# Transposes released by a small DMA on the sixth x tile, scalars without square roots on ScalarE, skip inputs loaded ahead of stores

## The chip, the cores and the metric

The kernel runs on one core of one Trainium2 chip. The metric is device time in microseconds (us) from start to end of one execution. A core has TensorE (PE in the profile; PEld is its weight loading), VectorE (DVE), ScalarE (ACT), GpSimd (POOL) and SyncE (SP). SP computes nothing here: it issues DMAs, and it issues them in the order of its queue, so that an issue that waits holds up all behind it.

## What is computed

A gate mixes two branches over the same input `x` of 2048 rows and 1024 columns, in bfloat16:

```python
g = sigmoid((x * gate_w).sum(-1, keepdims=True))
a = irfft2(rfft2(x) * (w_r + 1j * w_i))               # branch A: a filter in frequency
dt = exp(log_dt); Lam = Lambda_re + 1j * Lambda_im
Lam_bar = exp(dt * Lam)
B_bar = ((Lam_bar - 1.0) / Lam)[:, None] * Bmat
h[t] = Lam_bar * h[t - 1] + x[t] @ B_bar.T            # branch B: a state of 1024 complex numbers
b = 2.0 * real(h @ Cmat.T) + x * Dskip
out = g * a + (1 - g) * b
```

## The kernel before

**Branch A.** The Fourier transforms are matrix products with constant matrices. `fstage` (jj of 0 to 7) takes one x tile of 128 partitions x 2 x 1024: DVE forms sums and differences of halves (`eo`), POOL the few edge columns, and after every second tile PE does 4 groups of products into `ps_f`, each copied from PSUM into `big` (as `FX`) by two casts, L476 and L477. `fd`, `bf_w` and `bi` then go over 16 groups g of frequencies: forward along the columns (`ps_d`), forward along the rows (`ps_xe`, `ps_xo`), the product with the filter W on DVE, and back (`ps_q`). `idm` and `fi` transform back along the columns and write branch A's result to a scratch in HBM (`ya_scratch`). Each g needs a matrix MM that SP loads (L232) and a W that POOL loads.

**Branch B.** Time is cut into 4 chunks c of 512 steps, the 1024 states into 4 quarters q. `ssm_pe` multiplies x, transposed (`xT`), with B, transposed (`BT`), into `psu`; ACT scales the result by `rho` or `nrho` into `u`, of which there are two buffers. `ssm_dve` turns u by a phase from a table `tab`, runs four scans (L408), and turns the result back into `h`. A unit of this is one (c, q); there are 16. `tables(q)` makes the table of a quarter during chunk 0, from `thp`, `beta` and a ramp. `rho`, `nrho`, `thp`, `beta` and `r_sb` come from a chain of operations on 128 x 8 numbers (L278 to L344), with four table loads on ACT: for Exp, for Sin, for Sqrt, and for Sin and Arctan.

**Output.** For each tile tb of 128 rows, `half` multiplies h with C, transposed (`CT`), into `psy`, in two halves of 16 matmuls; L789 then forms `o` = psy x (1 - g) + `xf`, and SP stores it (L791). `xf` is prepared by `prep_d` (DVE: `xc` = x tile times Dskip, L760) and `prep_a` (ACT: `gac` = branch A's tile times g, L764; `xf` = xc times 1 - g, L766; POOL then adds gac to xf by an accumulating DMA, L767). At its end `prep_a` issues on SP the loads of xc and gac two tiles ahead. There are two buffers for xc and o, three for gac and xf.

**What sets the order.** Within the first stages SP and POOL, in the last stage ACT and SP, keep the order in which the program is written; the other engines' order is settled by a scheduler when the program is built, and each engine then runs its list in order. Two generators are merged by their planned times: branch A beside branch B's chunk 0 and part of the next, then branch B beside `c_all`, which writes out the order of the halves and what is prepared after each (`pre`).

**The start.** SP loads the x tiles, the first transform matrix `G_sb`, MM and W. Then come DMA transposes of B and of x. They are written after the fifth `fstage`; the first of them overwrites a place in BT into which POOL copies one column of the eighth x tile, so it must wait for that copy (L678):

```python
nc.gpsimd.tensor_copy(out=BT[:, 0, 0, 0, 0:1], in_=xts[7][:, 0, 0:1])
load_BT(0)
load_xT(0)
load_M(1)
...
```

Of the kernel before, what the change touches and what calls it, by code (L numbers as in the profile page):

```python
# [22 lines left out]
P = 128  # L23
# [113 lines left out]
def kernel(  # L137
# [137 lines left out]
    lre, lim, ldt = vec[:, 0, :], vec[:, 1, :], vec[:, 2, :]  # L275
    chpi = sp.tile([P, 1], FP32, name="chpi")
    nc.vector.memset(chpi, HALF_PI)
    dt = v8("dt")  # L278
    nc.scalar.activation(out=dt, in_=ldt, func=ACT.Exp)
    are = v8("are"); nc.vector.tensor_mul(out=are, in0=dt, in1=lre)  # L280
    r_sb = v8("r_sb")
    nc.scalar.activation(out=r_sb, in_=are, func=ACT.Exp)
    thp = v8("thp")
    nc.vector.scalar_tensor_tensor(out=thp, in0=lim, scalar=INV2PI, in1=dt, op0=ALU.mult, op1=ALU.mult)

    def frac(xx, n, nm, pool=sp, tag=None):
        kk = pool.tile([P, n], FP32, name=nm + "_k", **({"tag": tag} if tag else {}))
        nc.vector.tensor_scalar(out=kk, in0=xx, scalar1=MAGIC, scalar2=-MAGIC, op0=ALU.add, op1=ALU.add)
        nc.vector.tensor_sub(out=xx, in0=xx, in1=kk)
        nc.vector.tensor_scalar(out=kk.bitcast(I32), in0=xx.bitcast(I32), scalar1=0x7FFFFFFF, scalar2=None,  # L290
                                op0=ALU.bitwise_and)
        return xx, kk

    ang = sp.tile([P, 16], FP32, name="ang")
    nc.vector.tensor_copy(out=ang[:, 0:8], in_=thp)
    nc.vector.tensor_scalar_mul(out=ang[:, 8:16], in0=thp, scalar1=float(TC))
    rr, ra = frac(ang, 16, "ang")
    snc = sp.tile([P, 2, 16], FP32, name="snc")

    den = v8("den"); nc.vector.tensor_mul(out=den, in0=lre, in1=lre)  # L300
    den2 = v8("den2"); nc.vector.tensor_mul(out=den2, in0=lim, in1=lim)
    nc.vector.tensor_add(out=den, in0=den, in1=den2)
    inv = v8("inv"); nc.vector.reciprocal(out=inv, in_=den)
    nc.scalar.activation(out=snc[:, 0, :], in_=rr, func=ACT.Sin, scale=TWO_PI_LO)
    nc.scalar.activation(out=snc[:, 1, :], in_=ra, func=ACT.Sin, scale=-TWO_PI_LO, bias=chpi)
    sth, cth, sTC, cTC = snc[:, 0, 0:8], snc[:, 1, 0:8], snc[:, 0, 8:16], snc[:, 1, 8:16]
    sg = sp.tile([P, 8, 2], FP32, name="sg")
    nc.vector.tensor_scalar_mul(out=sg[:, :, 1], in0=sTC, scalar1=-1.0)
    nc.vector.tensor_copy(out=sg[:, :, 0], in_=sTC)
    lbi = v8("lbi"); nc.vector.tensor_mul(out=lbi, in0=r_sb, in1=sth)  # L310
    nr = v8("nr"); nc.vector.tensor_mul(out=nr, in0=r_sb, in1=cth)
    nc.vector.tensor_scalar_add(out=nr, in0=nr, scalar1=-1.0)
    t_a = v8("t_a"); nc.vector.tensor_mul(out=t_a, in0=nr, in1=lre)
    t_b = v8("t_b"); nc.vector.tensor_mul(out=t_b, in0=lbi, in1=lim)
    cr = v8("cr"); nc.vector.tensor_add(out=cr, in0=t_a, in1=t_b)
    t_c = v8("t_c"); nc.vector.tensor_mul(out=t_c, in0=lbi, in1=lre)
    t_d = v8("t_d"); nc.vector.tensor_mul(out=t_d, in0=nr, in1=lim)
    ci = v8("ci"); nc.vector.tensor_sub(out=ci, in0=t_c, in1=t_d)
    m2 = v8("m2"); nc.vector.tensor_mul(out=m2, in0=cr, in1=cr)
    m3 = v8("m3"); nc.vector.tensor_mul(out=m3, in0=ci, in1=ci)  # L320
    nc.vector.tensor_add(out=m2, in0=m2, in1=m3)
    mag = v8("mag")
    nc.scalar.activation(out=mag, in_=m2, func=ACT.Sqrt)
    rho = v8("rho")
    nc.vector.scalar_tensor_tensor(out=rho, in0=mag, scalar=2.0, in1=inv, op0=ALU.mult, op1=ALU.mult)
    nrho = v8("nrho")
    nc.vector.tensor_scalar_mul(out=nrho, in0=rho, scalar1=-1.0)
    hd = v8("hd"); nc.vector.tensor_add(out=hd, in0=mag, in1=cr)
    nc.vector.tensor_scalar_max(out=hd, in0=hd, scalar1=1e-30)
    nc.vector.reciprocal(out=hd, in_=hd)  # L330
    ht = v8("ht"); nc.vector.tensor_mul(out=ht, in0=ci, in1=hd)
    nc.vector.tensor_scalar(out=ht, in0=ht, scalar1=-1e15, scalar2=1e15, op0=ALU.max, op1=ALU.min)
    hq = v8("hq"); nc.vector.tensor_mul(out=hq, in0=ht, in1=ht)
    nc.vector.tensor_scalar_add(out=hq, in0=hq, scalar1=1.0)
    nc.scalar.activation(out=hq, in_=hq, func=ACT.Sqrt)
    nc.vector.tensor_scalar_add(out=hq, in0=hq, scalar1=1.0)
    nc.vector.reciprocal(out=hq, in_=hq)
    nc.vector.tensor_mul(out=ht, in0=ht, in1=hq)
    nc.scalar.activation(out=hd, in_=ht, func=ACT.Sin)
    fq = v8("fq")  # L340
    nc.scalar.activation(out=fq, in_=ht, func=ACT.Arctan)
    beta = v8("beta")
    nc.vector.tensor_scalar_mul(out=beta, in0=thp, scalar1=-255.5)
    nc.vector.scalar_tensor_tensor(out=beta, in0=fq, scalar=-2.0 * INV2PI, in1=beta, op0=ALU.mult, op1=ALU.add)  # L344

    tau_i = rp.tile([P, TC], I32, name="tau_i", tag="su")
    nc.gpsimd.iota(tau_i, pattern=[[1, TC]], base=0, channel_multiplier=0)
# [2 lines left out]

    def tables(q):
        xa = rp.tile([P, 2 * TC], FP32, name="xa", tag="cu")
        for jj in range(2):
            jb = 2 * q + jj
            xj = xa[:, TC * jj:TC * (jj + 1)]
            if q < 2:
                nc.vector.tensor_scalar(out=xj, in0=tau_f, scalar1=thp[:, jb:jb + 1], scalar2=beta[:, jb:jb + 1],
                                        op0=ALU.mult, op1=ALU.add)
            else:
                nc.scalar.activation(out=xj, in_=tau_f, func=ACT.Identity, scale=thp[:, jb:jb + 1],  # L360
                                     bias=beta[:, jb:jb + 1])
        rr, ra = frac(xa, 2 * TC, "xa", rp, "su")
        tq = tab[:, 2 * q:2 * q + 2]
        rr = rr.rearrange("p (a t) -> p a t", a=2)
        ra = ra.rearrange("p (a t) -> p a t", a=2)
        nc.scalar.activation(out=tq[:, :, 0, :], in_=ra, func=ACT.Sin, scale=-TWO_PI_LO, bias=chpi)
        nc.scalar.activation(out=tq[:, :, 1, :], in_=rr, func=ACT.Sin, scale=-TWO_PI_LO)
        nc.vector.tensor_scalar_mul(out=tq[:, :, 2, :], in0=tq[:, :, 1, :], scalar1=-1.0)


    hs = {}
# [71 lines left out]
    def fstage(jj):  # L443
# [10 lines left out]
        nc.gpsimd.tensor_sub(out=eo[:, :, 1, 1, 0:1], in0=om, in1=eo[:, :, 1, 0, 0:1])  # L454
        nc.gpsimd.tensor_add(out=eo[:, :, 1, 0, 0:1], in0=om, in1=eo[:, :, 1, 0, 0:1])
        eos[jj] = eo
        if jj % 2 == 0:
            return
        j0 = 2 * jj - 2
        for eo_i in range(2):  # L460
            for b in range(2):
                ps = psF.tile([P, 4, 2, P], FP32, name="ps_f", tag="ps")
                bs = slice(P * b, P * (b + 1))
                for jl in range(4):
# [9 lines left out]
                                     start=False, stop=True)  # L474
                q = 4 * eo_i + 2 * b
                nc.scalar.copy(out=FX[:, q, :, j0:j0 + 4], in_=ps[:, :, 0, :].rearrange("p j c -> p c j"))  # L476
                (nc.vector.tensor_copy if (eo_i, b) in ((1,0),(1,1)) else nc.scalar.copy)(  # L477
                    out=FX[:, q + 1, :, j0:j0 + 4], in_=ps[:, :, 1, :].rearrange("p j c -> p c j"))
                yield 1.0

# [193 lines left out]
    for jj in range(8):  # L674
        for _ in fstage(jj):
            pass
        if jj == 4:
            nc.gpsimd.tensor_copy(out=BT[:, 0, 0, 0, 0:1], in_=xts[7][:, 0, 0:1])  # L678
            load_BT(0)
            load_xT(0)  # L680
            load_M(1)
            load_W(1)
            load_BT(1)
            load_M(2)
            nc.sync.dma_start(out=FI_sb, in_=cFI)
            load_BT(2)
            load_BT(3)

    def ssm_all():
        prev = iter(())  # L690
        for c in range(NCH):
            for q in range(4):
                if c == 0:
                    tables(q)
                u = up.tile([P, 2, 2, TC], BF16, name="u", tag="u")
                for i, _ in enumerate(ssm_pe(c, q, u)):
                    yield 0.5
                    for _ in range((0,4,3,3)[i]):
                        next(prev, None)
                        yield 0.52  # L700
                prev = ssm_dve(c, q, u)
        for _ in prev:
            yield 0.72
# [29 lines left out]
    with ExitStack() as bctx:  # L733
# [59 lines left out]
        def c_all():  # L793
            order = [(0, 0), (1, 0), (2, 0), (0, 1), (1, 1), (2, 1)] + [(tb, dh) for tb in range(3, 16) for dh in range(2)]
            pre = {(0, 0): [(prep_d, 0), (prep_d, 1)], (1, 0): [(prep_a, 0)], (2, 0): [(prep_a, 1)],
                   (0, 1): [(prep_d, 2)], (1, 1): [(prep_a, 2)], (2, 1): [(prep_d, 3)], (3, 0): [(prep_a, 3), (prep_d, 4)],
                   (3, 1): [(prep_a, 4)]}
            for n in range(5, 16):
                pre[n - 1, 0] = [(prep_d, n)]
                pre[n - 1, 1] = [(prep_a, n)]  # L800
            for tb, dh in order:
                half(tb, dh)
                for f, n in pre.get((tb, dh), ()):
                    f(n)
                yield 3.6

        while ssm.t < 48:
# [38 lines left out]
```

## Time and profile before

| | |
|---|---|
| median of 6 runs | 353.71 us (351.27 to 356.54) |
| the profiled execution | 351.27 us |
| its span, first to last instruction | 349.5 us |
| mean granted TensorE clock | 0.993 |
| PE busy | 324.0 us (93%) |
| DVE busy | 297.6 us (85%) |
| ACT busy | 188.1 us (54%) |
| POOL busy | 42.2 us (12%) |

Times inside the execution are counted from the start of the span. Busy time of PE is modelled from pipelined matmuls, so that a busy PE is not PE at its peak. A wait is put down to what came last of all that the instruction waited for. In the row of activity each digit is the busy share of one fortieth of the span, in tenths.

### The profile page before, as it was taken

Reading aid. Unit: us, or ns where it says so; the run is one execution under the profiler, and the core shown is the slowest. Engines: PE = TensorE matmul, PEld = TensorE weight load, DVE = VectorE, ACT = ScalarE, POOL = GpSimd, SP = SyncE. Lnnn points to the kernel's source line nnn. Section 1 sums busy time; section 2 is a strip of 40 time slices with the busy share of each in tenths; the row PEclk is TensorE's granted clock in tenths of the full one; section 3 lists DMA queues with packets and bytes.
Section 4 is the critical chain, followed back from the end, with each engine's and each line's share of the span. In section 5 each row is a group of like instructions: output and inputs, shape, how many; then the busy total and the mean of one; then the engine's idle time right before and its main releaser. Section 6 shows DMA issues by size and latency. Waiting matters only on the chain.

```text
span 349.5 us, 4890 instructions
## 1 busy us (share of the span) xinstructions
PE 324.0 (93%) x1804; PEld 172.9 (49%) x1804; DVE 297.6 (85%) x419; ACT 188.1 (54%) x255; POOL 42.2 (12%) x89
## 2 busy tenths in 40 slices
PE   3788999799979999999999999999989898999995
PEld 1675666466646566554444444444434343444442
DVE  4998859978999969898999999989799798987431
ACT  1997979689948877596262426242322404322430
POOL 5330422122110000000011000000000000000110
PEclk9999999999989999999999999999999999999999
DMA  7899997989694121113994145223523223454863
GB/s 279 342 138 217 220 249 192 188 182 202 179 222 90 71 112 62 60 60 137 239 251 128 37 143 148 64 90 84 128 55 96 92 60 113 99 143 130 266 200 105
DMA packets 68169, 51.30 MB, mean 147 GB/s; under 512 B 52657, under 2 KB 55729, under 8 KB 68145
## 3 DMA queue, kind: packets, MB, share of 16 engines
q1 hardware_dynamic: 64144, 38.75, 44.7%
q0 software_dynamic: 3648, 12.07, 14.1%
q8 instruction: 14, 0.23, 0.3%
q10 hardware_dynamic: 352, 0.17, 0.2%
q14 instruction: 11, 0.08, 0.1%
HBM read 21.61 MB, written 8.39 MB: 86 GB/s over the span
## 4 chain that ended last, share of the span: by engine, by line
PE 56%; DVE 21%; DMA 9%; ACT 8%; issue 4%; SPq 2%; POOL 0%; DVEq 0%; ACTq 0%; POOLq 0%
PE psy L782 26%; PE psu L388 19%; DVE su L408 7%; DMA xc<-in_A_x_dram 3%; PE ps_id L557 3%; DVE cu L403 2%; DVE cu L433 2%; ACT X L500 2%; DMA CT<-in_A_x_dram 2%; DMA xT<-in_A_x_dram 1%; PE ps_d L488 1%; DMA MM<-c_MM 1%; DVE o L789 1%; ACT u L390 1%; ACT X L515 1%
## 5 line engine op out<-in xcount | busy, mean ns | idle before, releaser
L388 PE MATMUL psu<-xT,BT 128*128 128x512 bf16 x512 | 120.5, 379 | 5.9 <-ACT u L390 4.5
L388 PEld LDWEIGHTS <-BT 128*128 128x128 bf16 x512 | 49.7, 98 | 61.7 <-issue 7.6
L408 DVE TENSOR_TENSOR_SCAN su<-r_sb,carry,cu 128x512 bf16<-128x512 f32 x48 | 57.7, 1265 | 0.4
L390 ACT ACTIVATE u<-psu,rho 128x512 bf16<-128x512 f32 x32 | 22.1, 690 | 65.5 <-PE psu L388 35.5
L767 POOL DMA_DIRECT2D xf<-gac x16 | 14.0, 872 | 216.8 <-ACT xf L766 203.8
L782 PEld LDWEIGHTS <-h 128*128 128x128 bf16 x256 | 25.0, 98 | 30.2
L390 ACT ACTIVATE u<-psu,nrho 128x512 bf16<-128x512 f32 x32 | 22.1, 691 | 29.0 <-PE psu L388 29.0
L764 ACT ACTIVATE gac<-gac,gf 128x1024 bf16<-128x1024 bf16 x16 | 18.3, 1142 | 27.8 <-DMA gac<-ya_scratch 27.8
L782 PE MATMUL psy<-CT,h 128*128 128x512 bf16 x128 | 28.9, 379 | 0.0
L782 PE MATMUL psy<-big,h 128*128 128x512 bf16 x128 | 28.9, 379 | 0.0
L760 DVE TENSOR_TENSOR xc<-xc,dsk_bc 128x1024 bf16<-128x1024 bf16 x16 | 11.0, 687 | 18.5 <-DMA xc<-in_A_x_dram 18.5
L789 DVE SCALAR_TENSOR_TENSOR o<-psy,om_f,xf 128x1024 bf16<-128x1024 f32 (+1 forms) x17 | 20.6, 1215 | 6.9 <-PE psy L782 6.9
L399 DVE TENSOR_TENSOR cu<-u,tab 128x2048 bf16<-128x2048 bf16 x16 | 19.5, 1220 | 5.1 <-ACT u L390 5.1
L550 ACT CAST big<-ps_q 128x1024 bf16<-128x1024 f32 x16 | 16.4, 1027 | 10.2 <-PE ps_q L549 10.1
L782 PEld LDWEIGHTS <-big 128*128 128x128 bf16 x128 | 12.5, 98 | 15.1
L782 PEld LDWEIGHTS <-xT 128*128 128x128 bf16 x128 | 12.5, 98 | 15.1
L546 PE MATMUL ps_q<-MM,Y 128*128 128x256 bf16 x64 | 15.7, 279 | 4.6 <-DVE Y L527 4.6
L403 DVE TENSOR_TENSOR cu<-cu,su 128x2048 bf16<-128x2048 bf16 x16 | 19.6, 1226 | 0.3
L433 DVE TENSOR_TENSOR cu<-su,tab 128x2048 bf16<-128x2048 bf16 x16 | 19.5, 1220 | 0.1
L435 DVE TENSOR_TENSOR u<-su,tab 128x2048 bf16<-128x2048 bf16 x16 | 19.5, 1220 | 0.0
L401 DVE TENSOR_TENSOR su<-u,tab 128x2048 bf16<-128x2048 bf16 x16 | 19.5, 1219 | 0.0
L488 PE MATMUL ps_d<-G_sb,big 128*128 128x256 bf16 (+3 forms) x128 | 18.8, 286 | 0.0
(168 smaller groups left out, 558.8 us busy)
## 6 DMA issues: line engine op xcount, KB each, us to landing
xf<-gac POOLq DMA_DIRECT2D x16, 512.0 KB, 3.9
ya_scratch<-ya SPq DMA_DIRECT2D x16, 256.0 KB, 2.0
xc<-in_A_x_dram SPq DMA_DIRECT2D x16, 256.0 KB, 2.9
gac<-ya_scratch SPq DMA_DIRECT2D x16, 256.0 KB, 3.0
out_dram<-o SPq DMA_DIRECT2D x15, 256.0 KB, 2.0
MM<-c_MM SPq DMA_DIRECT2D x16, 192.0 KB, 3.9
xt<-in_A_x_dram SPq DMA_DIRECT2D x4, 512.0 KB, 4.2
CT<-in_A_x_dram SPq DMA_DIRECT2D x4, 512.0 KB, 8.0
```

The costliest lines, as they stand in the source:

```text
L388: nc.tensor.matmul(psu, lhsT=BT[:, jb, ri, dblk, :], rhs=xT[:, dblk, TC * c:TC * (c + 1)], start=(dblk == 0), stop=(dblk == 7))
L390: nc.scalar.activation(out=u[:, jj, ri, :], in_=psu, func=ACT.Copy, scale=(nrho if ri else rho)[:, jb:jb + 1])
L399: nc.vector.tensor_mul(out=cu, in0=u, in1=tq[:, :, 0:1, :].to_broadcast(full))
L401: nc.vector.tensor_mul(out=su, in0=u[:, :, ::-1, :], in1=tq[:, :, 1:3, :])
L403: nc.vector.tensor_add(out=cu, in0=cu, in1=su)
L408: nc.vector.tensor_tensor_scan(out=su[:, jj, ri, :], data0=r_sb[:, jb:jb + 1].to_broadcast([P, TC]), data1=cu[:, jj, ri, :], initial=(0.0 ...
L433: nc.vector.tensor_mul(out=cu, in0=su, in1=tq[:, :, 0:1, ::-1].to_broadcast(full))
L435: nc.vector.tensor_mul(out=u, in0=su[:, :, ::-1, :], in1=tq[:, :, 1:3, ::-1])
L488: nc.tensor.matmul(ps[:, lo:lo + w], lhsT=FX[:, q, 8 * g:8 * g + 8, :], rhs=G_sb[:, o:o + w], start=start, stop=stop, skip_group_check=True)
L764: nc.scalar.activation(out=gac, in_=gac, func=ACT.Copy, scale=gf[:, tb:tb + 1])
L782: nc.tensor.matmul(psy[:, ds], lhsT=hs[c, jb // 2][:, jb % 2, ri, P * tq:P * (tq + 1)], rhs=CT[dh][:, jb, ri, :], start=(i == 0), stop=(i ...
L789: nc.vector.scalar_tensor_tensor(out=o[:, ds], in0=psy[:, ds], scalar=om_f[:, tb:tb + 1], in1=xfs[tb][:, ds], op0=ALU.mult, op1=ALU.add)
```

## The change

*Release.* The POOL copy goes; instead SP moves 16 numbers of one partition of the sixth x tile into BT by a DMA, ahead of the transposes.

*Scalars.* The chain is rewritten as a generator `scalars()`, of which one step is taken before the first `fstage` and one in each of the following. The two Sqrt activations are replaced by an inverse square root on DVE (a first value from the bits of the number, then two Newton steps), the half-angle formula changes so that one Sin goes too, real and imaginary parts are handled in one operation of 16 columns, and a few operations move to POOL (`nrho`, a first `beta`, `sg`, the squared modulus).

*Casts.* In `fstage` the second cast of each group is always ACT's; before, DVE did it in two of the four.

*Tables.* `tables(q)` becomes a generator that treats its two halves of 512 columns one after the other.

*Skip inputs.* In `c_all` what is prepared comes before a `half` and no longer after it, and from tile 4 on `prep_a(n)` and `prep_d(n + 1)` stand together at (n - 1, 1). The loads that `prep_a` issues so stand on SP ahead of the store of that half's tile.

```diff
+    def rsqrt(y, x, s):
+        nc.vector.tensor_scalar(out=y.bitcast(I32), in0=x.bitcast(I32), scalar1=-0.5, scalar2=float(0x5F3759DF),
+                                op0=ALU.mult, op1=ALU.add)
+        for _ in range(2):
+            nc.vector.tensor_mul(out=s, in0=y, in1=y)
+            nc.vector.scalar_tensor_tensor(out=s, in0=s, scalar=-0.5, in1=x, op0=ALU.mult, op1=ALU.mult)
+            nc.vector.scalar_tensor_tensor(out=y, in0=s, scalar=1.5, in1=y, op0=ALU.add, op1=ALU.mult)
...
-    nc.scalar.activation(out=mag, in_=m2, func=ACT.Sqrt)
+        rsqrt(rs, m2, s)
+        nc.vector.tensor_mul(out=mag, in0=m2, in1=rs)
+        yield
+        nc.vector.scalar_tensor_tensor(out=rho, in0=mag, scalar=2.0, in1=inv, op0=ALU.mult, op1=ALU.mult)
+        nc.gpsimd.tensor_scalar_mul(out=nrho, in0=rho, scalar1=-1.0)
...
-    nc.scalar.activation(out=hq, in_=hq, func=ACT.Sqrt)
...
-    nc.scalar.activation(out=hd, in_=ht, func=ACT.Sin)
...
+    chain = scalars()
+    for _ in range(1):
+        next(chain, None)
...
     def tables(q):
         xa = rp.tile([P, 2 * TC], FP32, name="xa", tag="cu")
+        kk = rp.tile([P, 2 * TC], FP32, name="xa_k", tag="su")
+        tq = tab[:, 2 * q:2 * q + 2]
         for jj in range(2):
...
+            nc.scalar.activation(out=tq[:, jj, 0, :], in_=kj, func=ACT.Sin, scale=-TWO_PI_LO, bias=chpi)
+            nc.scalar.activation(out=tq[:, jj, 1, :], in_=xj, func=ACT.Sin, scale=-TWO_PI_LO)
...
         eos[jj] = eo
+        for _ in range(1):
+            next(chain, None)
...
-                (nc.vector.tensor_copy if (eo_i, b) in ((1,0),(1,1)) else nc.scalar.copy)(
+                (nc.vector.tensor_copy if (jj, eo_i, b) in () else nc.scalar.copy)(
...
         if jj == 4:
-            nc.gpsimd.tensor_copy(out=BT[:, 0, 0, 0, 0:1], in_=xts[7][:, 0, 0:1])
+            nc.sync.dma_start(out=BT[0:1, 0, 0, 0, 0:16], in_=xts[5][0:1, 0, 0:16])
             load_BT(0)
...
-                   (0, 1): [(prep_d, 2)], (1, 1): [(prep_a, 2)], (2, 1): [(prep_d, 3)], (3, 0): [(prep_a, 3), (prep_d, 4)],
-                   (3, 1): [(prep_a, 4)]}
-            for n in range(5, 16):
-                pre[n - 1, 0] = [(prep_d, n)]
-                pre[n - 1, 1] = [(prep_a, n)]
+                   (0, 1): [(prep_d, 2)], (1, 1): [(prep_a, 2)], (2, 1): [(prep_d, 3)], (3, 0): [(prep_a, 3), (prep_d, 4)]}
+            for n in range(4, 16):
+                pre.setdefault((n - 1, 1), []).append((prep_a, n))
+                if n < 15:
+                    pre.setdefault((n - 1, 1), []).append((prep_d, n + 1))
             for tb, dh in order:
-                half(tb, dh)
                 for f, n in pre.get((tb, dh), ()):
                     f(n)
+                half(tb, dh)
                 yield 3.6
```

More of the change, by code (lines that the diff above doesn't have):

```diff
@@ L277 @@
     nc.vector.memset(chpi, HALF_PI)
[L278 to L287, printed above, removed]
+    r_sb, beta, rho, nrho = (v8(n) for n in ("r_sb", "beta", "rho", "nrho"))
@@ L288, in frac @@
+    ang = sp.tile([P, 16], FP32, name="ang")
+    angk = rp.tile([P, 2, 16], FP32, name="angk", tag="cu")
+    snc = sp.tile([P, 2, 16], FP32, name="snc")
+    thp = ang[:, 0:8]
+    sTC, cTC = snc[:, 0, 8:16], snc[:, 1, 8:16]
+    sg = sp.tile([P, 8, 2], FP32, name="sg")
+    lam = scr[:, 28:30, :]
+    def frac(xx, kk, ff):
         nc.vector.tensor_scalar(out=kk, in0=xx, scalar1=MAGIC, scalar2=-MAGIC, op0=ALU.add, op1=ALU.add)
-        nc.vector.tensor_sub(out=xx, in0=xx, in1=kk)
-        nc.vector.tensor_scalar(out=kk.bitcast(I32), in0=xx.bitcast(I32), scalar1=0x7FFFFFFF, scalar2=None,
+        nc.vector.tensor_sub(out=ff, in0=xx, in1=kk)
+        nc.vector.tensor_scalar(out=kk.bitcast(I32), in0=ff.bitcast(I32), scalar1=0x7FFFFFFF, scalar2=None,
@@ L291, in frac @@
                                 op0=ALU.bitwise_and)
[L292 to L322, printed above, removed]
-    nc.scalar.activation(out=mag, in_=m2, func=ACT.Sqrt)
[L324 to L334, printed above, removed]
-    nc.scalar.activation(out=hq, in_=hq, func=ACT.Sqrt)
@@ L336, with v16 @@
-    nc.vector.tensor_scalar_add(out=hq, in0=hq, scalar1=1.0)
-    nc.vector.reciprocal(out=hq, in_=hq)
-    nc.vector.tensor_mul(out=ht, in0=ht, in1=hq)
-    nc.scalar.activation(out=hd, in_=ht, func=ACT.Sin)
[L340 to L344, printed above, removed]
+    def v16():
+        scr_n[0] += 2
+        return scr[:, scr_n[0] - 2:scr_n[0], :]
@@ new lines, in rsqrt, with scalars @@
+    def rsqrt(y, x, s):
[5 more added lines that the diff above has]
+            nc.vector.scalar_tensor_tensor(out=y, in0=s, scalar=1.5, in1=y, op0=ALU.add, op1=ALU.mult)
+    def scalars():
+        dt, are = v8("dt"), v8("are")
+        nc.scalar.activation(out=dt, in_=ldt, func=ACT.Exp)
+        nc.vector.scalar_tensor_tensor(out=thp, in0=lim, scalar=INV2PI, in1=dt, op0=ALU.mult, op1=ALU.mult)
+        nc.vector.tensor_scalar_mul(out=ang[:, 8:16], in0=thp, scalar1=float(TC))
+        frac(ang, angk[:, 0, :], angk[:, 1, :])
+        nc.scalar.activation(out=snc[:, 0, :], in_=angk[:, 1, :], func=ACT.Sin, scale=TWO_PI_LO)
+        nc.scalar.activation(out=snc[:, 1, :], in_=angk[:, 0, :], func=ACT.Sin, scale=-TWO_PI_LO, bias=chpi)
+        nc.vector.tensor_mul(out=are, in0=dt, in1=lre)
+        nc.scalar.activation(out=r_sb, in_=are, func=ACT.Exp)
+        yield
+        dd, inv = v16(), v8("inv")
+        nc.gpsimd.tensor_mul(out=dd, in0=lam, in1=lam)
+        nc.gpsimd.tensor_add(out=dd[:, 0, :], in0=dd[:, 0, :], in1=dd[:, 1, :])
+        nc.vector.reciprocal(out=inv, in_=dd[:, 0, :])
+        yield
+        nl, pr, c2 = v16(), v16(), v16()
+        nc.vector.tensor_mul(out=nl, in0=snc[:, ::-1, 0:8], in1=r_sb.unsqueeze(1).to_broadcast([P, 2, 8]))
+        nc.vector.tensor_scalar_add(out=nl[:, 0, :], in0=nl[:, 0, :], scalar1=-1.0)
+        nc.vector.tensor_mul(out=pr, in0=nl, in1=lam)
+        nc.vector.tensor_add(out=c2[:, 0, :], in0=pr[:, 0, :], in1=pr[:, 1, :])
+        nc.vector.tensor_mul(out=pr, in0=nl[:, ::-1, :], in1=lam)
+        nc.vector.tensor_sub(out=c2[:, 1, :], in0=pr[:, 0, :], in1=pr[:, 1, :])
+        yield
+        m2, rs, mag, s = v8("m2"), v8("rs"), v8("mag"), v8("s")
+        nc.vector.tensor_mul(out=pr, in0=c2, in1=c2)
+        nc.vector.scalar_tensor_tensor(out=m2, in0=pr[:, 0, :], scalar=1e-30, in1=pr[:, 1, :], op0=ALU.add, op1=ALU.add)
+        rsqrt(rs, m2, s)
+        nc.vector.tensor_mul(out=mag, in0=m2, in1=rs)
+        yield
+        nc.vector.scalar_tensor_tensor(out=rho, in0=mag, scalar=2.0, in1=inv, op0=ALU.mult, op1=ALU.mult)
+        nc.gpsimd.tensor_scalar_mul(out=nrho, in0=rho, scalar1=-1.0)
+        hd = v8("hd")
+        nc.vector.tensor_add(out=hd, in0=mag, in1=c2[:, 0, :])
+        nc.vector.tensor_scalar_max(out=hd, in0=hd, scalar1=1e-20)
+        nc.vector.tensor_mul(out=m2, in0=hd, in1=mag)
+        yield
+        rsqrt(rs, m2, s)
+        nc.vector.tensor_mul(out=m2, in0=m2, in1=rs)
+        nc.vector.scalar_tensor_tensor(out=hd, in0=m2, scalar=float(np.sqrt(2.0)), in1=hd, op0=ALU.mult, op1=ALU.add)
+        nc.vector.reciprocal(out=hd, in_=hd)
+        yield
+        nc.vector.tensor_mul(out=hd, in0=c2[:, 1, :], in1=hd)
+        nc.vector.tensor_scalar(out=hd, in0=hd, scalar1=-1.0, scalar2=1.0, op0=ALU.max, op1=ALU.min)
+        fq = v8("fq")
+        nc.scalar.activation(out=fq, in_=hd, func=ACT.Arctan)
+        nc.gpsimd.tensor_scalar_mul(out=beta, in0=thp, scalar1=-255.5)
+        nc.vector.scalar_tensor_tensor(out=beta, in0=fq, scalar=-2.0 * INV2PI, in1=beta, op0=ALU.mult, op1=ALU.add)
+        nc.gpsimd.tensor_scalar_mul(out=sg[:, :, 1], in0=sTC, scalar1=-1.0)
+        nc.gpsimd.tensor_copy(out=sg[:, :, 0], in_=sTC)
+        yield
@@ L352, in tables @@
         xa = rp.tile([P, 2 * TC], FP32, name="xa", tag="cu")
+        kk = rp.tile([P, 2 * TC], FP32, name="xa_k", tag="su")
+        tq = tab[:, 2 * q:2 * q + 2]
         for jj in range(2):
             jb = 2 * q + jj
-            xj = xa[:, TC * jj:TC * (jj + 1)]
+            xj, kj = xa[:, TC * jj:TC * (jj + 1)], kk[:, TC * jj:TC * (jj + 1)]
             if q < 2:
@@ L358, in tables @@
                                         op0=ALU.mult, op1=ALU.add)
+                yield
             else:
@@ L361, in tables @@
                                      bias=beta[:, jb:jb + 1])
[L362 to L367, printed above, removed]
+            nc.vector.tensor_scalar(out=kj, in0=xj, scalar1=MAGIC, scalar2=-MAGIC, op0=ALU.add, op1=ALU.add)
+            yield
+            nc.vector.tensor_sub(out=xj, in0=xj, in1=kj)
+            nc.vector.tensor_scalar(out=kj.bitcast(I32), in0=xj.bitcast(I32), scalar1=0x7FFFFFFF, scalar2=None,
+                                    op0=ALU.bitwise_and)
+            yield
+            nc.scalar.activation(out=tq[:, jj, 0, :], in_=kj, func=ACT.Sin, scale=-TWO_PI_LO, bias=chpi)
+            nc.scalar.activation(out=tq[:, jj, 1, :], in_=xj, func=ACT.Sin, scale=-TWO_PI_LO)
         nc.vector.tensor_scalar_mul(out=tq[:, :, 2, :], in0=tq[:, :, 1, :], scalar1=-1.0)
+        yield
     hs = {}
@@ L693, in ssm_all @@
                 if c == 0:
-                    tables(q)
+                    for _ in tables(q):
+                        yield 0.0
                 u = up.tile([P, 2, 2, TC], BF16, name="u", tag="u")
```

## The prediction

> **What bounds the kernel now.** I read the activity rows first: which engine is full, and where.
>
> ```profile
> PE   3788999799979999999999999999989898999995
> ...
> DVE  4998859978999969898999999989799798987431
> ACT  1997979689948877596262426242322404322430
> ```
>
> A slice is 8.74 us. TensorE (PE) is full from slice 13 (105 us) on; only slices 30, 32 and 34 dip to 8. Before slice 5 (35 us) it is not full. So time can come from two places: the dips near 250 to 290 us, and the start. The stretches of ten us show the dips' size, and the waits of 195 to 320 us their names (us, times, longest):
>
> ```profile
> 250.00:260.00 10.00, 8.32 (x39) 3.70 (x38) 9.93 (x12) 1.95 (x3) 0.00 (x0) 1.00 0.20 49
> ...
> 270.00:280.00 10.00, 9.09 (x43) 4.06 (x42) 7.86 (x8) 4.03 (x5) 0.87 (x1) 1.00 0.25 80
> 280.00:290.00 10.00, 8.08 (x39) 3.59 (x37) 9.90 (x9) 1.49 (x3) 0.00 (x0) 1.00 0.22 53
> ```
>
> ```profile
> DVE xc L760 <- DMA xc<-in_A_x_dram: 8.5, 6, 2.3
> ...
> PE psu L388 <- ACT u L390: 4.5, 3, 1.9
> ```
>
> The second column is PE: 1.68 + 0.91 + 1.92 = 4.5 us idle, the three waits of the last line. ACT's `u` was late because its buffer comes free only with `h` of the unit two before, and DVE was late with that. Why DVE was late stands in the chain of waits, once per tile:
>
> ```profile
> 241.95 1.28 DVE o L789
> 243.25 0.34 SPq L791
> ...
> 243.68 4.05 DMA xc<-in_A_x_dram
> ...
> 247.76 0.69 DVE xc L760
> ```
>
> DVE makes output tile n, SP stores it, only then does SP issue the load of xc(n+3), and DVE multiplies that tile two operations after the output: it waits for a load that its own output held back. Six such waits, 8.5 us of DVE.
>
> At the start, the timeline has what the other parts touch:
>
> ```profile
> 10.05 1.28 ACT L304 ACT_TABLE_LOAD   x1
> ...
> 17.25 0.44 POOL L678 COPY BT<-CT 128x1 bf16<-128x1 bf16 x1 [2.74 <-DMA CT<-in_A_x_dram]
> ...
> 17.71 1.33 SPq L211 DMA_TRANSPOSE BT<-in_B_B_re_dram  x1
> ...
> 29.02 0.38 PE L388 MATMUL psu<-xT,BT 128*128 128x512 bf16 x1 [1.41 <-DMA xT<-in_A_x_dram]
> ```
>
> One table load of ACT costs 1.28 us. POOL waits for the eighth x tile (17.25), and its copy frees SP's transposes (17.71); the second half of xT lands at 28.9 and PE has waited 1.41 us for it.
>
> **Skip loads ahead of stores: -4.5 us.** In the built order of SP, the load of xc(n+3) now stands before the store of tile n, behind the store of n-1. It still needs the buffer of xc(n+1), so ACT's `xf`(n+1). For xc(7): the store of tile 3 was issued at 228.2, `xf`(5) ended at 234.4; with 0.4 us of issue and the longest landing, 4.05, it is there at 238.9. DVE wants it after o(4), which ended at 243.2: 4.3 us to spare. For xc(8) `xf`(6) ended at 248.2, so 252.7 against 259.5. DVE's multiply moves from two operations behind the output to right behind it, 2.3 us earlier; the spare covers that, and without it each tile would stall again by what is missing. The gac load, issued with it, moves alike; the store now waits for ACT, but was due later anyway: the output has two buffers, and a tile comes only each 14 us.
>
> Are the PE gaps then gone? One unit and one output tile cost PE 64 matmuls at 3.45/16 us = 13.8 us. Starts of L403 on DVE are 201.55, 216.53, 232.09, 248.37, 263.47, 279.36, 294.10: six steps of 14.98, 15.56, 16.28, 15.10, 15.89, 14.74. The first PE gap (259) came after three of them, when DVE had fallen 46.82 - 41.4 = 5.4 us behind; the gap was 1.7, so 3.7 us were slack. Less the waits of 7.5 us in these steps, all six together fall behind by only 92.55 - 7.5 - 82.8 = 2.3 us. That is inside the slack, so all 4.5 us go. What is late next is PE itself: its order in this stage is unchanged. I take 4.5; bounds 2.5 (one gap stays) and 4.5 (there is no more idle PE between 160 and 345).
>
> **Release by a small DMA: -0.3 us.** The POOL copy (0.44) becomes a 32-byte DMA on SP that waits for tile 6, and the transposes wait for its landing. What SP holds behind it: all transposes of BT and xT, then MM and W. When does it land? From issue plus landing: MM 6.71 + 7.2 = 13.9, W 15.6 and 15.9, tile 8 at 9.21 + 8.0 = 17.2: landings follow issues. Tile 6 went out just ahead of MM, so it lands at about 13.3 (an estimate from MM's 192 KB at the page's 340 GB/s). The Trainium skill ("DMA: Bandwidth & Descriptors", section "Anatomy of one DMA") puts a fixed 2.0 us on a DMA (fitted on the GpSimd path): landing at 15.4, transposes 2.3 us earlier. The same page's section on queues, rings and completion order says that each engine takes its descriptors in ring order: then the small DMA stands behind tile 7, W and tile 8, whose data fill the engines until 16.4, and lands with the latter at about 17.4. The four landings above speak for the second: I take 17.4, against 17.71: -0.3. Bounds: -2.3, and +1.5 (it needs its 2.0 us after tile 8's 17.2).
>
> POOL loses its wait for tile 8, which held tile 6's edge columns until 17.6. But it gains one: in the built order `nrho` stands ahead of tile 5's edges, and its `rho` comes on DVE after tile 7's first addition (lands near 15.2). With DVE's 0.34 us per addition I put rho at 16.8; then 1.0 us on POOL for each tile's edges: tile 6 ready at 19.2. So cover is exchanged for cover.
>
> **Scalars and casts in the forward stage: about 0.** ACT drops two table loads (four become two), two Sqrt and one Sin, and takes over eight casts from DVE. By the rows: -2 x 1.28 - 3 x 0.12 + 8 x 0.48 = +0.9 us of ACT; DVE -8 x 0.62 = -5.0, plus about as many tiny operations as it loses (0.08 each, up to 0.19 where one needs the last). The skill ("ScalarE: Activation LUTs", "What ACT_TABLE_LOAD costs") counts 2.66 us for a switch, load and drain: ACT -1.8. But the row ends a cast at 10.03 and starts the load at 10.05; I see no drain and take 1.28. ACT then has 32 casts in a row; the third group can't start before tile 6's edges (19.4), and two groups of 8 at 0.48 and the arctangent end at 27.4, where DVE's last cast now ends at 27.97. The built PE order puts the first two forward groups wholly ahead of `psu`, so they no longer stand behind the xT wait: the first ps_xe, at 31.04 now, comes after xT (28.6) and five psu matmuls, near 29.8. That 1.2 us is not kept: the fifth ps_xe waits for MM, whose load SP issues at 42.33, after the transposes, landing at 47.12. SP is busy with them from 17.7 to 54; it gains the 0.3 of the release and the 0.3 (37.57 to 37.89) by which it waited for PE. So -0.6 passes. The tables now run in halves: for q of 2 and 3 that adds some 0.1 to 0.2 us on DVE and 0.1 on ACT for each, +0.3 where these are the bound (54 to 110). Sum of the front: -0.3, release included; bounds -2.3 and +2.5.
>
> **Sum.** -4.5 - 0.3 = -4.8. The profiled execution took 351.27 us (span 349.5 and 1.77 around it), so 346.5. The median of the six runs is 353.71; the same difference gives **348.9 us**, 1.4% less.
>
> **Rivals.**
> - *The release is really early* (fixed landing, no ring order). For it: small loads on ACT's queue landed within 4 us under load. Against: the four landings. Another -2.0: 344.5, or 346.9 on the median. Chance 0.06.
> - *The PE gaps stay, or return under another name*: `psu` still waits for `u`, since DVE with 13.8 to 14.5 us per unit is no faster than PE. For: DVE's row is at 9 until 318. Against: the 2.3 of 3.7 us above. Only the front remains: 351.0, or 353.4. Chance 0.2.
> - *The front loses 1 to 2.5 us* (a late landing or a longer ACT row) beside the full gain: 348.5, or 351.0. Chance 0.07.
> - *Slower: POOL's edges stand behind a late rho.* Everything of the third group waits for it; the last cast is rho + 10.6 us, the first ps_xe some 2.4 later, so from rho at 18.0 on each us costs one, and from 22.5 on the 4.5 are eaten. At 25: +7.0 - 4.5, so 353.8, or 356.2. For: 22 small operations in series, each waiting for the last. Against: in the present rows such operations are 0.08 to 0.19 apart, which puts rho near 17. Chance 0.1.
>
> **From cases to numbers.** About 1% (3.5 us) is what a measurement of this kernel can tell from no change. Forecast 0.57 (a few of its outcomes stay under 1%), early release 0.06: faster 0.6; the second and third rival and the forecast's edge: same 0.28; the last and the worst of the second: slower 0.12. The range takes in the early release with room for scatter (345.0), and the second rival (353.4) at the other end.
>
> **What would show it.** In the new profile: no wait of L784 (the xc multiply) for its load before 310 us; the three `psu <- u` waits gone and PE without a gap from 160 to the end; SP's first transpose at 17.3 to 17.6 and xT landing near 28.6; two ACT table loads before 30 us, and the last forward cast near 27.4. Wrong: a first transpose at 15.5 or 19, a PE gap over 1 us after 200, or POOL's `nrho` later than 18.

## The result, and the profile after

The changed kernel takes **350.23 us** (median of 20 runs, 347.10 to 352.93); the kernel before, on the same chip, 353.12 us (41 runs). The ratio is 0.9906 [0.9885, 0.9927]. In a second comparison (below) it was 0.9866 [0.9818, 0.9915]. Medians are over all executions, while ratios use only those within 1.5% of the fastest of the same kernel, so a ratio is not the quotient of the two medians. Medians apart: 2.9 and 5.4 us; forecast: 4.8. The profiled execution took 346.58 us (span 344.8) against 351.27 (349.5): 4.7 us apart.

The rows of activity of the changed kernel, in 40 slices of 8.62 us:

```profile
PE   2979899899979899999999999999999999999995
DVE  2879758997999979898999999999999999996321
ACT  3789979779849787687344314423424424423400
```

The dips of PE near 250 to 290 us are gone: from 121 us (slice 15 of 40) on it is full, but for the last slice. The same stretches of ten us as before (second column: PE busy; third: its weight loads; fourth: DVE):

```profile
250.00:260.00 10.00, 10.00 (x48) 4.49 (x46) 9.90 (x13) 2.47 (x4) 0.00 (x0) 1.00 0.43 126
...
270.00:280.00 10.00, 10.00 (x48) 4.57 (x47) 9.90 (x10) 4.15 (x6) 0.86 (x1) 1.00 0.35 100
280.00:290.00 10.00, 10.00 (x48) 4.51 (x46) 9.90 (x10) 4.03 (x5) 0.00 (x0) 1.00 0.20 59
```

PE executes 48 matmuls in each stretch, where it had 39, 43 and 39. And the waits of DVE between 195 and 320 us (us, times, longest); PE has none left there:

```profile
DVE xc L784 <- DMA xc<-in_A_x_dram: 3.3, 1, 3.3
```

The one that is left ends at 317.5 us, behind the last unit of branch B, where DVE has nothing else to do. The load of xc(7), issued at 243.68 and landed at 247.74 before, was now issued at 234.75 and landed at 237.18, and DVE multiplied it at 242.45 without a wait. The chain of waits shows the change of bound (before, then after; q marks an engine's own queue, so SPq is SP issuing DMAs), and at the start how the release went (start, length, what):

```profile
PE 56%; DVE 21%; DMA 9%; ACT 8%; issue 4%; SPq 2%; POOL 0%; DVEq 0%; ACTq 0%; POOLq 0%
```

```profile
PE 69%; DVE 10%; SPq 6%; DMA 6%; ACT 5%; issue 2%; ACTq 0%; DVEq 0%
```

```profile
6.30 7.44 DMA CT<-in_A_x_dram
13.81 3.86 DMA BT<-CT
17.68 1.34 SPq L211
...
38.59 4.57 DMA MM<-c_MM
43.20 0.28 PE ps_xe L534
```

DVE fell from 21% of the chain to 10%, since DVE, SP and the xc load no longer alternate in it once per tile. Tile 6 landed at 13.74, but its 32-byte DMA needed 3.86 us, and SP's first transpose starts at 17.68, where it started at 17.71. The two late lines say that PE's fourth ps_xe now waits for the load of MM, which SP issues at 38.59 (37.89 before).

Three points of time cut the span up. First psy of the output stage: 167.53 us before, 167.88 after. End of the last psy: 345.36 and 340.71. So **the output stage is 177.83 - 172.83 = 5.00 us shorter, and all ahead of it 0.35 us longer.** The 0.35 us is a difference of two single executions, and the first psy moves by more than that from one execution of a kernel to the next: with the front and the release of before it starts at 167.53, 168.75, 168.76 and 170.53 us in four profiles (two of them with the new loads), in a second profile of the changed kernel at 170.41.

### The profile page after: what moved, and what is told of

Read it like the earlier page. It is cut to its first block, busy times and chain, and to the rows that moved or that the text cites. A ratio compares the mean times of both kernels' runs of the same rounds, so it can differ in the third digit from the quotient of the medians.

```text
span 344.8 us, 4922 instructions
## 1 busy us (share of the span) xinstructions
PE 323.4 (94%) x1804; PEld 173.2 (50%) x1804; DVE 294.9 (86%) x424; ACT 190.2 (55%) x266; POOL 44.1 (13%) x94
## 4 chain that ended last, share of the span: by engine, by line
PE 69%; DVE 10%; SPq 6%; DMA 6%; ACT 5%; issue 2%; ACTq 0%; DVEq 0%
PE psy L806 32%; PE psu L409 26%; SPq L211 3%; DVE su L429 3%; PE ps_id L580 3%; DMA CT<-in_A_x_dram 2%; SPq L216 2%; DMA MM<-c_MM 1%; DMA vec<-in_B_Lambda_im_dram 1%; DVE t L549 1%; DMA BT<-CT 1%; PE ps_y L599 1%; DVE su L422 1%; PE ps_d L511 1%; PE ps_y L602 1%
## 5 line engine op out<-in xcount | busy, mean ns | idle before, releaser
L788 ACT ACTIVATE gac<-gac,gf 128x1024 bf16<-128x1024 bf16 x16 | 18.2, 1140 | 11.1 <-DMA gac<-ya_scratch 11.1
L790 ACT ACTIVATE xf<-xc,om_f 128x1024 f32<-128x1024 bf16 x16 | 18.3, 1142 | 8.5 <-DVE o L813 6.0
```

The source lines that it names most:

```text
L790: nc.scalar.activation(out=xf, in_=xc, func=ACT.Copy, scale=om_f[:, tb:tb + 1])
```

## The experiments

Line numbers are those of the kernel that an experiment starts from. Each line of runs below gives medians, and the ratio to the kernel before, measured beside it.

### The two halves of the change

The order of `c_all` alone, in the kernel before:

```diff
             for tb, dh in order:
-                half(tb, dh)
                 for f, n in pre.get((tb, dh), ()):
                     f(n)
+                half(tb, dh)
```

(with the new `pre`). 

> The kernel before with only the order of the skip loads taken from the change. Theory (all of the gain is the three PE gaps of the output stage): the profiled execution lies 4.5 to 5.0 us under the 351.3 us of before, at 346.3 to 346.8 us; no psu wait for u, PE without a gap from 160 us to the end; ratio to before about 0.990, that of the whole change (0.9906). Rival (the front's edits carry part of it): a gain of 3 us or less, and the rest in the run that changes the front alone.

Measured: 348.16 us against 355.06, ratio 0.9817 [0.9774, 0.9859]; profiled execution 347.52, 0.7 over the range named, with the forward stage starting 0.5 us later than in the changed kernel's; no wait of `psu` for `u`, output stage 172.83 us.

The other half, the changed kernel with the old `c_all`:

> The changed kernel with only the old order of the skip loads put back, so the front's edits alone. Theory: the front costs 0.3 us as in the trace of the changed kernel, a profiled execution at 351.3 to 351.9 us, ratio 0.999 to 1.003, the three waits of psu for u back with 4 to 5 us. Rival: the front gains 0.5 us or more (ratio under 0.998).

Measured: 355.20 against 355.06, ratio 1.0007 [0.9970, 1.0044]; output stage 177.79 us. Its profiled execution, with three drops of the clock (below), took 357.99 us, far over the 351.9 I had named. The waits are back:

```profile
PE psu L409 <- ACT u L411: 4.5, 3, 2.2
```

So the loads carry all of the gain that can be told from noise: the output stage takes 172.83 us, to 0.01, in all eleven profiles with the new order of loads, 177.8 in two of the three with the old one and 180.24 in the third (below). The front alone changes nothing beyond its interval, about 1.3 us either way. The gain of the loads by the first run's ratio is larger than forecast. It was repeated later, beside other kernels:

> The kernel before with the new order of the skip loads alone, once more, beside the other three on one chip. Theory: ratio 0.980 to 0.985, so 2 us above the early copy and 1 to 3 us under the changed front with nrho on DVE. Rival (its first ratio was luck): 0.986 to 0.990, level with the whole change.

Measured: 348.94 against 352.82, ratio 0.9879 [0.9828, 0.9930], output stage 172.82 us. This lies in the rival's band, so the first ratio was in part luck, though the interval takes in the theory's band as well. Two ratios of the loads alone (0.9817 and 0.9879) and two of the whole change (0.9906 and 0.9866) do not tell the two apart.

### What the release is worth

Two variants of the kernel before with the new loads. In the first, POOL's copy waits for the sixth tile and not for the eighth; in the second the line is gone:

```diff
-            nc.gpsimd.tensor_copy(out=BT[:, 0, 0, 0, 0:1], in_=xts[7][:, 0, 0:1])
+            nc.gpsimd.tensor_copy(out=BT[:, 0, 0, 0, 0:1], in_=xts[5][:, 0, 0:1])
```

> Before with the new order of the skip loads, and POOL's one-element copy that frees the transposes reads the sixth x tile instead of the eighth: a release at 14.2 to 14.7 us without a DMA in it. Theory (the small DMA gained nothing since it landed behind the queue; SP's row of transposes sets the pace until 54 us): the first transpose starts 3 us earlier, at about 14.6, the fifth ps_xe follows 1 to 3 us earlier than 47.2, and the time falls 1 to 3 us under that of the loads alone. Rival (the transposes only wait in the same rings behind the x tiles, or delay tile 8): the first transpose is issued at 14.6, but the second half of xT still lands near 28.6, or tile 8 lands later than 17.2, and the time is within 0.5 us of the loads alone.

> The same with no release at all: SP issues the transposes right behind the load of the eighth x tile, from 9.6 us on. Theory (ring order keeps the tiles ahead of the transposes): tile 8 lands within 0.5 us of 17.2, all transposes are 3 to 8 us earlier, and the time is 1 to 4 us under that of the loads alone. Rival (transposes slow the loads beside them): tile 8 lands over 1 us later, the last forward cast is later than 28 us, and the time is no better than that of the loads alone, or worse.

Measured, beside the loads alone (348.16): 346.08 us, ratio 0.9760 [0.9722, 0.9799], and 347.28 us, 0.9785 [0.9743, 0.9828]. SP's transposes in the profile of the first, then of the second:

```profile
15.93 1.33 SPq L211 DMA_TRANSPOSE BT<-in_B_B_re_dram  x1
17.30 1.47 SPq L211 DMA_TRANSPOSE BT<-in_B_B_im_dram  x1
18.82 6.25 SPq L216 DMA_TRANSPOSE xT<-in_A_x_dram  x2
```

```profile
12.12 2.67 SPq L211 DMA_TRANSPOSE BT<-in_B_B_re_dram  x1
14.84 4.52 SPq L211 DMA_TRANSPOSE BT<-in_B_B_im_dram  x1
19.41 5.54 SPq L216 DMA_TRANSPOSE xT<-in_A_x_dram  x2
```

With the loads alone the first started at 18.55, so with the copy of tile 6 it is 2.6 us earlier (15.93, where 14.6 was named); PE's waits for xT (1.5 us) and MM are gone and the fifth ps_xe comes at 47.15 instead of 48.32. The theory's 1 to 3 us hold in the medians (2.1); the spans of the two profiles, with one drop of the clock each (below), are 1.0 us apart. Without a release SP starts at 12.12, but its first two transposes take 2.67 and 4.52 us instead of 1.3, and xT's go out 0.6 us later than with the copy. Issued into the stream of x loads, they gain nothing over a release at tile 6. Two signs of the rival appeared as well: tile 8 landed at 19.51 (18.25 with the loads alone), and the last forward cast started at 31.38 (28.17). So the time ends between theory and rival: 0.9 us under the loads alone.

### Where the clock drops

The times of one kernel lie 6 us apart, and the first comparison's medians are closer than its profiles. The column of the granted clock says in part why. In windows of two us it is 1.00, or falls to 0.50 for 3.4 us; one such drop in a span of 345 us makes a mean of 0.995, two 0.990, three 0.985, and every run lists its mean. A second look at the kernel before, one execution:

> The kernel before, unchanged, for a second profile. In the profiles so far the granted clock drops to 0.5 for about 3.4 us at a time and is 1.0 otherwise; one such drop makes the mean 0.995, two 0.990, three 0.985, and each costs PE about 1.7 us where PE is the bound. Theory (a drop follows when PE, having waited for 1.5 to 2.4 us, is full again): with a mean clock of 0.990 or less this profile shows its additional drop right behind one of PE's waits (for xT near 29 us, for Y near 72, or for u at 259 to 292). Rival (drops fall anywhere): it lies in a stretch where PE had not waited for 5 us.

Measured: 356.72 us, clock 0.990, and the additional drop stands at 265.6 us. One of PE's waits, and the windows around it (second column PE, third from the end the clock):

```profile
264.65 2.65 PE L388 MATMUL psu<-xT,BT 128*128 128x512 bf16 x8 [2.27 <-ACT u L390]
```

```profile
262.00:264.00 2.00, 0.38 (x2) 0.10 (x1) 1.97 (x3) 0.09 (x1) 0.00 (x0) 1.00 0.00 0
264.00:266.00 2.00, 1.35 (x6) 0.63 (x6) 2.00 (x2) 1.18 (x2) 0.00 (x0) 0.91 0.09 30
266.00:268.00 2.00, 2.00 (x7) 0.66 (x5) 1.26 (x2) 0.67 (x2) 0.00 (x0) 0.50 1.02 309
268.00:270.00 2.00, 2.00 (x8) 0.79 (x7) 1.72 (x2) 2.00 (x3) 0.00 (x0) 0.74 0.15 58
```

PE waited 2.27 us for `u`, was full again, and a microsecond later its clock was halved: only 7 matmuls in two us. Its output stage took 180.24 us, 7.4 more than with the new loads: 5.1 of idle time, 0.6 by which the profile understates four gaps (see "Why the prediction was right"), and 1.7 of the drop. A drop in the run of the front alone:

```profile
46.00:48.00 2.00, 1.54 (x9) 1.11 (x10) 0.06 (x1) 0.74 (x1) 0.00 (x0) 0.74 1.21 321
48.00:50.00 2.00, 2.00 (x6) 0.76 (x5) 1.91 (x3) 0.00 (x0) 0.24 (x1) 0.50 1.19 303
50.00:52.00 2.00, 2.00 (x17) 1.34 (x15) 0.83 (x3) 1.31 (x2) 0.93 (x2) 0.91 0.91 186
```

It follows PE's wait of 2.43 us for MM, ended at 46.46. Over all 14 profiles there are 21 drops between 15 and 340 us, each starting (read in windows of half a microsecond) from 0.2 us before to 1.5 us after the end of a PE wait of at least 1.2 us; of such waits there are 48, so not every one brings a drop. The one near 99 us for Y (the product with W, made by DVE; 2.2 to 2.9 us) has one in 13 of 14.

What decides stands in the same traces. In each of them the clock changes lie whole multiples of 3.41 us apart, to a thousandth, so that each execution has a fixed grid of 3.41 us. Below are the stretch of that grid ahead of the drop above and the drop itself; then two stretches at the third gap of the first profile of before, which had no drop:

```profile
262.21:265.63 3.42, 1.15 (x6) 0.48 (x5) 3.39 (x4) 1.27 (x2) 0.00 (x0) 1.00 0.01 2
265.63:269.04 3.41, 3.41 (x10) 1.21 (x8) 2.39 (x4) 1.71 (x3) 0.00 (x0) 0.50 0.73 231
```

```profile
286.78:290.19 3.41, 1.49 (x8) 0.62 (x7) 3.38 (x3) 0.99 (x2) 0.00 (x0) 1.00 0.01 2
290.19:293.60 3.41, 3.41 (x17) 1.52 (x16) 2.47 (x4) 2.01 (x4) 0.00 (x0) 1.00 0.73 228
```

PE was busy for 34% of the first stretch, for 44% of the third. Over the 14 profiles, PE was busy for at most 41% of the stretch ahead of 19 of the drops, for 47% ahead of the other two (both in the forward stage); of the 1312 other stretches between 15 and 340 us the lowest has 44%. So a wait brings a drop when enough of it falls into one stretch of the grid, and where the grid lies differs between executions. An estimate from these shares: where PE is otherwise full, that takes 2.0 us of waiting (59% of 3.41) inside one stretch.

### The front's two new waits

The changed kernel again, and with MM in four buffers, so that MM(3) is loaded ahead of the third block's transposes:

```diff
-        m = fr.tile([P, 6, P], BF16, name="MM", bufs=3)
+        m = fr.tile([P, 6, P], BF16, name="MM", bufs=4)
...
             load_M(2)
+            load_M(3)
...
-            if g + 3 < 16:
-                load_M(g + 3)
+            if g + 4 < 16:
+                load_M(g + 4)
```

> The changed kernel, unchanged, timed again beside the two next. Theory (its front has a wait for MM of 0.9 to 2.4 us more, behind which the clock drops): clocks of 0.985 to 0.990 in most runs, ratio to before 0.988 to 0.992 where the loads alone gave 0.982. Rival (the first comparison was a matter of the chip): clocks of 0.995 in most runs, ratio 0.980 to 0.984.

> The changed kernel with four buffers for MM in place of three: the load of MM(3) goes out before the transposes of the third block instead of behind them, each later one a group earlier. Theory (PE's wait for MM near 43 us costs its own 0.9 us and, in most executions, a drop of the clock behind it): no wait of ps_xe for MM, clocks at 0.990 to 0.995 in most runs, 1.5 to 3 us less than the changed kernel beside it. Rival (that wait is covered later, at the waits for Y near 72 and 98 us): within 0.7 us of the changed kernel, with the same clocks.

Measured: 350.14 us, ratio 0.9866 [0.9818, 0.9915], clocks from 0.980 to 0.995; and with four buffers 347.74 us, 0.9798 [0.9755, 0.9841], clocks 0.989 to 0.995, no wait of ps_xe for MM. 2.4 us under the kernel beside it, more than the 0.9 that the wait itself took, so the theory's size. The changed kernel's own ratio fell between my two bands, and half of its six runs had the clocks that I named. The changed kernel's profile has its additional drop not behind MM this time but at 22.8 us, behind 1.8 us of waits for POOL's edges. The next two take that wait away, the first with an early copy as well:

```diff
-        nc.gpsimd.tensor_scalar_mul(out=nrho, in0=rho, scalar1=-1.0)
+        nc.vector.tensor_scalar_mul(out=nrho, in0=rho, scalar1=-1.0)
...
-            nc.sync.dma_start(out=BT[0:1, 0, 0, 0, 0:16], in_=xts[5][0:1, 0, 0:16])
+            nc.gpsimd.tensor_copy(out=BT[:, 0, 0, 0, 0:1], in_=xts[5][:, 0, 0:1])
```

> The changed kernel with its small DMA replaced by POOL's one-element copy of the sixth tile, and nrho made on DVE, so that POOL has nothing ahead of that copy that waits for rho. Theory: the first transpose 2 to 3 us earlier than with the small DMA (15 to 16 instead of 17.7 to 18.6), no wait for MM, the third group of casts at about 19.5 instead of 21.0, and 2 to 4 us less than the changed kernel beside it, close to the ratio of 0.976 that the loads and such a copy alone gave. Rival (the changed front holds PE up in another place): less than 1 us under the changed kernel.

Measured: 347.81 us, ratio 0.9809 [0.9765, 0.9853]; the first transpose at 16.85 (15 to 16 was named), no wait for MM or POOL, casts of the third group in line with the second. The saving is the theory's (2.3 us); the ratio of the old front with the same copy (0.976) was missed.

The first line of that diff alone:

> The changed kernel with one operation moved: nrho is made on DVE instead of POOL, so POOL's edges of the fifth and sixth tile no longer stand behind rho. Theory (the new front's cost is the waits of PE behind POOL, 1.8 us at 19 to 22, and behind MM, each with a drop of the clock in some executions): no wait of ps_f for POOL, the third group of casts 1 to 1.5 us earlier, the last cast at 27.0 to 27.7 with the first x tile landing as early as in the changed kernel; the wait for MM grows by about as much, to 1 to 2.5 us, so the time stays within 1 us of the changed kernel (ratio 0.986 to 0.992). Rival (POOL's late edges alone are the front's cost): ratio 0.980 to 0.984.

Measured: 350.23 us, ratio 0.9925 [0.9895, 0.9955]. The last cast starts at 27.06 (28.24 in the changed kernel), but the waits of PE are now these:

```profile
PE ps_xe L534 <- DMA MM<-c_MM: 1.8, 1, 1.8
PE psu L409 <- DMA xT<-in_A_x_dram: 1.7, 1, 1.7
```

The ratio is just outside my band and its interval reaches into it; the mechanism is the theory's. A faster forward stage only reaches the transposes' row sooner, and waits there.

Last, both fronts with the early copy and four MM buffers:

> The kernel before with three edits: the skip loads ahead of the stores, POOL's copy that frees the transposes reading the sixth tile, and four buffers for MM. Theory (with the early release SP is no longer late with MM, so the fourth buffer adds nothing): within 0.7 us of that kernel without the fourth buffer, ratio about 0.976, clocks at 0.995. Rival: a further 1 us or more (ratio 0.973 or less).

> The changed kernel with POOL's copy of the sixth tile as the release, nrho on DVE and four buffers for MM: all that the runs so far found against the changed front. Theory: no wait of PE for MM, for POOL or for xT over 1 us; ratio 0.974 to 0.980, level with the old front and the early copy. Rival (the new scalars, casts and half tables are worth something once nothing hides them): 1 us or more under the old front with the early copy and four buffers, beside it.

Measured: old front 347.21 us, ratio 0.9831 [0.9783, 0.9879]; new front 348.25 us, 0.9858 [0.9811, 0.9904]. The old front's span is 344.5, with three buffers it was 344.7: the fourth adds nothing there. Its ratio missed my 0.976, on a chip where the kernel before was faster, and only three of its six runs had the clock I named (0.993 to 0.995; the others 0.990). The new front missed its 0.974 to 0.980 too, and kept a wait of 1.2 us for xT, where I had named none over 1 us. So it is no better than the old one even with the early copy and the fourth buffer: its rival, 1 us or more under the old front, did not come.

**The version that beats both kernels** is the kernel before with the new order of loads and the copy of the sixth tile: 346.08 us where the kernel before took 355.06, and 348.16 with the loads alone. It was not timed beside the changed kernel; against the kernel before its ratio is 0.9760 [0.9722, 0.9799], the changed kernel's 0.9906 and 0.9866.

## Why the prediction was right, and where its steps were off

**Skip loads ahead of stores: -4.5 forecast, -5.00 measured.** The mechanism came out as drawn: no L784 wait before 310 us but in DVE's free time, no `psu <- u` wait, PE without a gap, and loads alone reproduce it. The term was mis-sized by its upper bound, "there is no more idle PE". The idle column understates a gap: a matmul is drawn 0.379 us long where the next follows after 3.45/16 = 0.216, so 0.163 us of the last one ahead of a gap count as busy. Three gaps of 4.51 us in all cost 4.51 + 3 x 0.163 = 5.00. The second term missed is the clock: a gap may cost 1.7 us more behind it, as in the second look at before.

**Release: -0.3 forecast, -0.03 measured.** The choice between fixed cost and ring order was right: it landed with tile 8, not 2.0 us after 13.74. In all five profiles with the small DMA the first transpose starts 0.17 to 0.19 us behind tile 8's landing, in the four with POOL's copy of the eighth tile 0.30 to 0.51. So the 0.3 was gained (0.51 became 0.18 between the two first profiles), but tile 8 itself landed 0.3 later in that execution, 17.50 against 17.20. That this is the release's fault, and not that of the transposes behind it, is shown by the copy of the sixth tile: 2.6 us earlier and 2.1 us gained. The early-release rival had the right prize and the wrong instruction.

**Scalars.** Two table loads before 30 us, as forecast. But rho was put at 16.8 and came at 18.2. The last operations ahead of it are a square root in steps that each need the one before, 0.20 us apart (17.16, 17.36, 17.56), and not the 0.08 to 0.19 of the rows before. POOL and ACT in the changed kernel:

```profile
18.46 0.44 POOL L336 TENSOR_SCALAR nrho<-rho 128x8 f32<-128x8 f32 x1 [4.64 <-DVE scr L338]
18.86 0.40 POOL L473 TENSOR_TENSOR eo<-CT 128x2 bf16<-128x2 bf16 x1
```

```profile
20.98 0.59 ACT L499 CAST big<-ps_f 128x512 bf16<-128x512 f32 x1 [1.51 <-PE ps_f L496]
```

POOL waited 4.64 us for rho, the edges of the fifth tile stood behind it, and the third group of casts started at 20.98 instead of 19.4. The sign named for this, nrho later than 18, appeared: the last cast started at 28.24, so by the pitch of 0.48 us it ended at 28.7, forecast 27.4. The slope of the slower rival (from rho at 18 each us costs one) was too steep: moving nrho to DVE started the last cast 1.2 us earlier (27.06) and made the kernel no faster.

**First ps_xe and what passes.** Forecast 29.8, measured 30.55 (31.04 before). I let -0.6 pass at MM, taking SP's durations as they were. SP's row of transposes got slower: xT's two took 6.02 us (5.79), one of the third block 2.04 (1.52); MM(3) went out at 38.59, 0.7 later. From the first transpose to MM(3) SP took 20.9 to 23.1 us in the four profiles with the new front, the small DMA and three buffers, 19.7 to 21.1 in the four with the old front and POOL's copy of the eighth tile. So the half microsecond gained turned into a wait for MM. Front: -0.3 forecast, +0.35 measured between two single profiles, which is inside the scatter told above. Why SP's row is longer stays open, and the half tables (+0.3 forecast) were not tried alone. The copy of the sixth tile shows the bound from the other side: SP starts earlier, and the time falls.

**The median: 348.9 forecast, 350.23 measured.** Profile to profile the sum holds (-4.8 against -4.7), in part by luck: -5.00 and +0.35 stand where -4.5 and -0.3 were forecast, and both first profiles are the fastest execution of their series. By the ratios the time fell 0.9% in the first comparison and 1.3% in the second; the forecast, 348.9 to 353.71 or 0.9864, lies in the second interval and not in the first.

The times follow the number of drops too: from the mean clocks, the kernel before has 1.9 a run (54 runs), the changed one 2.1 (27), the loads alone 1.3 (11), the old front with loads and early copy 1.2 (6). In the last comparison the runs of before averaged 351.3 us with one drop, 354.2 with two, 355.7 with three; the two without one took 351.9. The loads took away the places in the output stage, and the new front offers others. That a removed wait removes drops is supported by these counts, not shown. 1.9 drops against 2.1 are worth 0.3 us, so drops alone do not explain why the first comparison shows 2.9 us and not 5; as the intervals of the two comparisons overlap, I leave that open.

## What to carry to other kernels

Where an engine waits once per tile for a load that its own output holds back, move the load ahead of the store in the queue: that was all of the gain that could be told from noise. A tiny DMA was a poor signal behind a full queue: the first transpose started 11.3 to 12.0 us after the issue of tile 6's load; with POOL's one-element copy of the same tile it was 8.7 in the old front, 10.4 and 10.7 in the new one. Before shortening a stage, ask whether its successor is bound by another queue (here SP's transposes), because the time saved comes back as a wait, and a wait of some two microseconds on PE can cost 1.7 us more than itself.

## What was not expected of the hardware

- PE's granted clock is 1.00 or, for 3.4 us, 0.50, which costs 1.7 us of full work. All 21 drops start within 1.5 us of the end of a PE wait, on a grid of 3.41 us whose place differs between executions. The Trainium skill ("TensorE: Matmul & The Clock Gate", section "The HAM clock gate") has the halved clock follow an idle window of about 3.4 us. The length of the drops agrees; but here PE need not be idle for the whole window: the waits last 1.3 to 2.9 us, and PE was busy for 15% to 47% of the 3.41 us ahead of a drop. The measurement decides. So the wait's place decides along with its length: the wait for Y near 70 us, nearly as long as the one near 99, had a drop in 4 of 14 profiles.
- SP's first two transposes took 1.33 and 1.30 us when issued behind the landing of the x loads, as before, and 2.67 and 4.52 us when issued among them, as without a release.
- ACT's casts out of PSUM keep a pitch of 0.48 us for 22 in a row (with nrho on DVE, starts from 11.37 to 21.40), while the drawn length of each grows from 0.59 to 0.84 us: go by the starts.
